# Attention and MLP mixer on one core: first loads over two queues, a later zero fill, and another step list

## The chip, the cores and the metric

The kernel runs on one core of a Trainium2 chip. The metric is device microseconds (us) of one execution; lower is better. The core has five engines that work side by side: PE (TensorE, matrix products), DVE (VectorE), ACT (ScalarE), POOL (GpSimd) and SP (SyncE, which here only issues DMAs). Each engine works off its own instructions strictly in order, and an instruction that waits holds up all that follow on its engine. Sixteen DMA engines move the data. DMAs can be issued by SP, ACT and POOL, each of which has a queue of its own.

## The reference

All inputs are bf16; S = 2048 rows, D = 512, F = 1376.

```python
xn = layernorm(x)
# A: sliding-window attention, 32 heads of 16, 8 keys at distances 0,2,..,14
q, k, v = split(xn @ wqkv)
logits[s, w] = (q[s] . k[s - 2*w]) / 4          # masked where s - 2*w < 0
s = softmax(logits) applied to v[s - 2*w], then @ wo
# B: MLP on xn
h  = gelu(layernorm(xn) @ w1)
hs = concat(h[0:128] shifted by 1 row, h[128:256] by -1, h[256:384] by 2, h[384:] by -2) @ w2
x1 = xn + hs
g  = silu(x1 + gelu(layernorm(x1) @ w3) @ w4)
out = x + s * g
```

## The kernel before

The 2048 rows are 16 tiles of 128 rows in 4 chunks of 512. A chunk's rows are dealt out so that tile i of a chunk holds every fourth row, four tiles to a chunk. Almost all of the program is a list of named steps, the string `ORDER`. Each token is a call: `v.3.3` runs `v(3, 3)`, the last number being the PSUM bank for steps that have a matrix product. Nothing reorders them: the steps are issued in the order of the list, so the list fixes the order on every engine, and the waits follow from the data, from buffers that are used again, and from the DMA completion counters, of which eight for SP and ACT are used in turn.

The steps, by engine (i is a tile, c a chunk, k a pair of tiles):

- SP, DMAs: `ldxp` loads a pair of x tiles (256 KB), `ldxc` a chunk; `ldv` and `ldw1` load one half each of v's weights and of w1 (256 KB a half), `ldqk` the q or the k half of wqkv, `ldw2`, `ldw3`, `ldw4`, `ldwo` the other weights; `xT`, `hTr`, `x1Tr`, `oTr`, `tE` are DMA transposes; `vl` loads windows of v back from DRAM; `pre` copies x to the output, `so` and `soh` store a tile or half a tile.
- DVE: `st` takes a tile's statistics (two instructions), `nm0` and `nmv` normalise; `pw` multiplies q by a shifted k; `smx`, `sms`, `smn` do the softmax; `xa` adds w2's product, `nm3` normalises for w3; `vp` multiplies v windows by the weights; `ya` adds w4's product; `sg` multiplies by the attention's output; `gb`, `fav`, `sgh`, `favh` are the last tiles' multiply and add.
- ACT: `sqw` (a first square root, which loads its table), `sq0` (square root of the variance), `ev0h` and `ev0a` (evict transposes), `ev`, `eqk`, `eh`, `eg`, `eo`, `eoT`, `ge` (evict products, some with a gelu), `si` (silu), `nm` (normalise).
- POOL: `c_zero` writes 14 rows of zeros ahead of v in DRAM by a DMA and zeroes the edges of `hT`; `c_elog`, `c_sel`, `c_ident` build constants; `rs` and `r3` are reciprocal roots for a pair; `sv` stores v by a DMA; `soa` adds a tile onto the output by a DMA.
- PE: `warmup` (products on zeros), `tr0` (transposes of the first four tiles), `v`, `w1`, `w2`, `w3`, `w4`, `wo`, `woh` (half of one), `qk`, `lg` (logits), `ws` (window sums), `oTp` (transposes).

At the start PE transposes tiles 0 and 1 (`tr0.0`, `tr0.1`), multiplies them by v's weights and by w1, then turns to tiles 2 and 3. Tiles 4 and on come transposed by DMA. At the end tiles 0 to 11 are added onto x in DRAM by `soa`, tiles 12 to 15 are finished by DVE and stored.

The list before begins so (to the first product with v's weights):

```
ldxp.s.0 c_warm c_small warmup.10.512.0 sqw c_ident kh.0 ldv.s.0 ldv.s.1 ldxp.s.1 ldw1.s.0
ldw1.s.1 c_zero st.0 ldxp.s.2 ldxp.s.3 st.1 sq0.0 ldqk.s.0 ldqk.s.1 nm0.0 sq0.1 rp.0 nm0.1
tr0.0.0 warmup.8.128.1 ev0h.0.0 ev0h.0.1 st.2 tr0.1.2 v.0.1
```

Of the kernel before, what the change touches and what calls it, by code (L numbers as in the profile page):

```python
# [18 lines left out]
tr0.0.0 warmup.8.128.1 ev0h.0.0 ev0h.0.1 st.2 tr0.1.2 v.0.1 st.3 ev0h.1.0 ev0h.1.1 sq0.2 v.1.2
ev.0 nm0.2 sq0.3 rp.1 w1.0.0 ev.1 nm0.3 rs.0 sv.0 st.5 tr0.2.1 ldxc.s.2 w1.1.2 ev0a.2 sv.1 rr.0  # L20
st.4 tr0.3.3 rs.1 v.2.1 ev0a.3 st.7 rp.2 rs.2 w1.2.4 ev.2 st.6 eh.0 v.3.3 sv.2 rp.3 rr.1 w1.3.1
nmv.4 nmv.5 ev.3 qk.0.1.5 xT.2 eh.1 sv.3 qk.0.0.3 rs.3 qk.0.3.2 eh.2 eh.3 eqk.0.1 c_elog
qk.0.4.1 qk.0.5.5 nmv.6 nmv.7 st.11 ldxc.s.3 st.10 st.8 eqk.0.3 eqk.0.5 qk.0.2.2 eqk.0.0
qk.0.6.4 eqk.0.2 st.9 eqk.0.4 qk.0.7.3 eqk.0.6 eqk.0.7 pw.0.1 rp.5 st.15 st.13 rp.4 xT.3 hTr.0
ldw2.s hTr.1 w1.4.1 v.5.4 ldwo.s.0 ev.5 w1.5.3 v.4.2 ev.4 qk.1.4.4 rs.4 sv.4 v.6.5 w1.7.2 rr.3
rr.2 eh.4 pw.0.2 kh.1 ev.6 sv.5 rs.5 nb.4 pw.0.0 st.12 eqk.1.4 eh.5 w1.6.1 qk.1.1.4 qk.1.2.3
v.7.5 hTr.2 nm.8 nm.9 w2.1.0 pw.0.3 nb.5 rp.6 eh.6 xT.4 vl.s.1.1 eh.7 st.14 rp.7 lg.0.0 rs.7
eqk.1.2 lg.0.1 ev.7 pw.0.5 w2.0.5 rs.6 eqk.1.1 nm.11 nm.10 pw.0.4 sv.7 qk.1.5.4 sv.6 xT.5
qk.1.6.3 xa.1 nb.7 qk.1.0.2 nb.6 st3s.1 eqk.1.6 hTr.3 rr.4 xa.0 ldw3.s.0 st3s.0 eqk.1.5 pw.0.6
nm.13 nm.12 nm.15 qk.1.7.0 qk.1.3.4 w2.2.5 w1.9.3 w1.8.1 eh.9 eh.8 xa.2 rr.7 hTr.4 rr.5 rq.0  # L30
w1.10.5 pw.0.7 r3.0 v.8.3 eh.10 st3s.2 nm.14 w2.3.1 nm3.0 nm3.1 eqk.1.3 w2.5.5 ev.8 qk.2.0.4
xa.3 st3s.3 eqk.1.7 eqk.1.0 xT.6 lg.0.3 rq.1 kh.2 xa.5 lg.0.2 r3.1 w2.4.2 smx.0 ldw3.s.1 sv.8
xT.7 x1Tr.0 v.10.5 qk.2.4.0 w2.6.1 eqk.2.4 nm3.3 xa.4 ex.0 w2.7.3 w1.11.2 xa.6 st3s.6 nm3.2 xa.7
qk.2.5.1 eqk.2.0 x1Tr.1 eh.11 ev.10 sv.10 rr.6 v.9.0 v.11.3 w1.13.4 eqk.2.5 ev.9 hTr.5 qk.2.7.2
w1.15.1 eqk.2.7 w1.12.0 vl.s.2.0 vl.s.0.0 ldw4.s.2 qk.2.2.2 vl.s.3.1 eh.12 pw.1.0 st3s.4 st3s.7
st3s.5 v.12.5 eqk.2.2 pw.1.3 sms.0 eh.13 v.13.0 w3.0.6.4 ev.11 hTr.6 rq.2 qk.2.1.3 pw.1.2 r3.2
sv.9 eg.0.6 eqk.2.1 ldwo.s.3 smn.0 rq.3 pw.1.1 r3.3 w3.0.1.2 qk.2.3.4 w3.0.10.3 nm3.4 eqk.2.3
tE.0 eh.15 eg.0.10 ev.13 eg.0.1 lg.1.1 lg.1.0 pw.1.7 w2.8.1 w1.14.0 w3.0.0.2 eh.14 w3.0.2.3
hTr.7 qk.2.6.0 eqk.2.6 eg.0.0 w2.10.4 nm3.6 vl.s.0.1 nm3.7 x1Tr.3 vl.s.1.0 pw.1.5 xa.8 pw.1.4
nm3.5 pw.1.6 w2.11.1 xa.10 w3.0.8.2 xa.11 qk.3.1.4 st3s.11 eg.0.8 ev.12 w2.14.1 lg.1.2 st3s.10  # L40
sv.12 lg.1.3 eqk.3.1 w2.12.4 sv.11 st3s.8 eg.0.2 smx.1 w2.9.3 ldw4.s.1 x1Tr.2 xa.9 w2.15.5 xa.14
w3.0.3.2 w3.0.9.3 xa.12 pw.2.2 qk.3.2.1 qk.3.0.4 w2.13.0 st3s.9 eqk.3.2 eqk.3.0 eg.0.3 vl.s.9.1
ldw4.s.0 rq.4 xa.15 vl.s.9.0 vl.s.3.0 ldwo.s.2 pre.s.2 qk.3.3.1 w3.0.5.2 st3s.12 qk.3.4.5 eg.0.5
pw.2.3 eqk.3.3 qk.3.5.4 st3s.14 pw.2.4 xa.13 pw.2.1 rq.5 st3s.15 v.15.1 eqk.3.5 v.14.2 ev.15
eqk.3.4 w3.1.1.0 w3.0.4.5 vp.0 st3s.13 rq.6 pw.2.0 r3.4 nm3.9 w3.0.7.1 eg.0.4 ev.14 eg.0.9
eg.0.7 ex.1 qk.3.7.4 w3.1.0.2 eg.1.0 sv.14 r3.5 nm3.10 rq.7 nm3.11 x1Tr.5 w3.1.8.1 vl.s.2.1
pre.s.1 vl.s.10.0 vl.s.10.1 w4.1.3 eqk.3.7 ldwo.s.1 kh.3 sv.15 r3.7 c_sel sms.1 w4.0.5 w4.2.4
ya.0 smn.1 r3.6 w3.1.5.5 w4.3.2 nm3.8 ya.2 ya.1 vp.1 x1Tr.4 w3.1.9.3 nm3.15 eg.1.5 ya.3 w3.1.6.4
pre.s.0 vp.3 tE.1 w3.1.7.2 eg.1.6 eg.1.1 w3.1.3.5 w3.1.4.0 eg.1.7 vp.2 lg.2.1 lg.2.0 qk.3.6.2
eg.1.8 w3.1.10.1 eqk.3.6 nm3.14 pw.2.5 pw.2.7 w3.1.2.4 eg.1.3 eg.1.10 eg.1.4 lg.2.2 pw.2.6  # L50
x1Tr.7 eg.1.2 ws.2.1 ws.1.0 ws.0.4 eg.1.9 pw.3.2 ws.3.3 eo.1 lg.2.3 eo.0 smx.2 vl.s.4.1 w4.6.0
w3.2.0.4 oTr.0 eo.2 eo.3 oTr.1 vl.s.5.1 pw.3.0 ex.2 vl.s.4.0 vl.s.6.0 vl.s.5.0 w4.5.3 vl.s.6.1
ya.6 pw.3.4 w4.7.0 w4.4.1 w3.2.3.5 sms.2 si.2 si.1 si.3 eg.2.0 eg.2.3 si.6 vl.s.7.1 vl.s.7.0
pw.3.1 pw.3.5 nm3.12 ya.4 wo.1.4 nm3.13 ya.7 w3.2.2.1 sg.1 w3.2.9.0 vp.4 ya.5 w3.2.5.4 w3.2.4.5
eg.2.9 w3.2.1.2 smn.2 x1Tr.6 w3.2.8.0 vp.5 eg.2.4 eg.2.2 eg.2.5 w3.2.10.1 w3.2.7.4 w3.2.6.5
eg.2.7 eg.2.10 eg.2.1 eg.2.8 vp.6 tE.2 vl.s.8.1 vl.s.8.0 wo.0.3 eg.2.6 wo.2.1 wo.3.0 pw.3.3 sg.2
w4.10.5 soa.2 sv.13 sg.3 vp.7 w3.3.0.0 lg.3.0 eg.3.0 lg.3.2 si.4 pw.3.6 pw.3.7 ws.4.0 ws.5.1
lg.3.1 ws.7.2 ws.6.4 eo.4 ya.10 lg.3.3 vl.s.11.1 w4.9.0 smx.3 eo.5 si.7 si.0 eo.7 si.5 eo.6
si.10 vl.s.13.1 oTr.2 vl.s.13.0 vl.s.11.0 w4.8.2 vp.9 vl.s.12.1 ex.3 oTr.3 w4.11.4 ya.8 ya.9
sms.3 ya.11 smn.3 w3.3.7.0 w3.3.5.2 w3.3.1.5 eg.3.5 vp.10 tE.3 wo.4.4 eg.3.7 eg.3.1 vl.s.14.1  # L60
vl.s.12.0 sg.0 vl.s.14.0 vp.11 w3.3.4.1 w3.3.9.2 w3.3.10.5 eg.3.10 w3.3.8.0 w3.3.3.3 w3.3.6.5
eg.3.9 eg.3.4 vp.8 w3.3.2.1 eg.3.6 eg.3.8 wo.6.2 eg.3.2 eg.3.3 wo.7.0 sg.6 vp.13 ws.10.3 ws.9.2
eo.10 ws.11.1 ws.8.5 eo.9 w4.13.3 vl.s.15.0 sg.4 vl.s.15.1 vp.12 eo.11 eo.8 wo.5.4 si.11 oTr.5
vp.14 si.9 w4.12.5 oTr.4 w4.15.1 ya.12 sg.5 si.12 si.8 sg.7 vp.15 w4.14.0 soa.1 soa.0 soa.3
soa.7 soa.5 soa.4 soa.6 ya.13 ya.15 si.13 ws.13.4 ya.14 ws.15.3 ws.12.1 ws.14.5 eo.15 wo.8.0
si.14 eo.14 wo.9.3 sg.8 eo.12 eo.13 wo.10.1 soa.8 sg.9 si.15 oTp.13.4 soa.9 sg.10 oTp.14.3
eoT.13 oTp.12.0 wo.11.5 eoT.12 oTp.15.4 eoT.14 wo.13.0 eoT.15 wo.14.3 wo.12.4 woh.15.0.1
woh.15.1.2 soa.10 sg.11 soa.11 ge.13 gb.13 ge.14 fav.13 gb.14 so.s.13 ge.12 fav.14 gb.12 so.s.14
sgh.15.0 fav.12 favh.15.0 so.a.12 sgh.15.1 soh.s.15.0 favh.15.1 soh.a.15.1
# [805 lines left out]
```

## Time and profile before

| what | value |
|---|---|
| median of 3 runs | 190.26 us (189.74 to 190.42) |
| profiled execution, its own time | 190.75 us |
| its span in the profile | 189.0 us |
| granted TensorE clock, mean | 0.996 |
| busy, share of the span | PE 97%, DVE 87%, ACT 60%, POOL 23% |
| DMA, moved | 39.25 MB, mean 208 GB/s |

How to read it: the span runs from the program's first recorded instruction to its last, and 1.75 us of the profiled execution lie around it. Times in the views count from the span's start. "[1.44 <-DMA xc<-in_A_x_dram]" behind a row says that the engine had been idle for 1.44 us before it and that the landing of x ended this idle time. A line such as L333 is a line of the kernel before. A matrix product's recorded end is modelled, so PE is best read by the starts of its rows.

### The profile page before, as it was taken

To read this page: it belongs to the slowest core of one execution; us is meant where nothing else is said; L and a number is where in the kernel's file an instruction comes from. 1 tells how busy PE (TensorE), PEld (TensorE's weight loads), DVE (VectorE), ACT (ScalarE), POOL (GpSimd) and SP (SyncE) were. 2 spreads that over 40 slices of the span, in tenths; PEclk is the share of its full clock that TensorE was granted. 3 is DMA by queue.
4 is the path that set the end of the run, shared out by engine and by line. 5 is a ranking of instruction groups with operands and counts; after the bars stand their busy time and mean duration, and the time that the engine had idled before them with its cause. 6 is when DMAs were issued, how large, how long until landed. Compare 5 with 4: busy or idle time off the path is not lost.

```text
span 189.0 us, 3685 instructions
## 1 busy us (share of the span) xinstructions
PE 182.8 (97%) x1430; PEld 87.0 (46%) x1430; DVE 165.1 (87%) x270; ACT 112.8 (60%) x189; POOL 42.7 (23%) x70
## 2 busy tenths in 40 slices
...
GB/s 164 315 352 115 199 248 141 194 238 137 233 120 286 278 64 224 222 87 190 399 162 361 274 57 134 254 401 277 189 190 95 254 335 238 210 254 106 88 106 116
DMA packets 47842, 39.25 MB, mean 208 GB/s; under 512 B 35251, under 2 KB 41889, under 8 KB 47777
## 3 DMA queue, kind: packets, MB, share of 16 engines
...
q10 hardware_dynamic: 288, 0.20, 0.3%
...
HBM read 26.41 MB, written 5.78 MB: 170 GB/s over the span
## 4 chain that ended last, share of the span: by engine, by line
PE 85%; DMA 4%; DVE 4%; issue 2%; POOL 2%; SPq 1%; ACT 1%; POOLq 0%
PE mm L668 20%; PE mm L685 18%; PE mm L443 15%; PE mm L611 8%; PE mm L496 7%; PE mm L471 6%; PE lg L543 4%; PE mm L768 4%; DMA xc<-in_A_x_dram 3%; PE mm L729 3%; POOL out_dram L835 2%; DMA out_dram<-xr 1%; DVE st L333 1%; DVE xr L775 1%; DVE xr L786 1%
## 5 line engine op out<-in xcount | busy, mean ns | idle before, releaser
L530 DVE TENSOR_TENSOR pw<-qT,kT 128x2048 bf16<-128x2048 bf16 x32 | 38.3, 1214 | 3.4 <-PE lg L543 2.4
L668 PE MATMUL mm<-x1T,w_sb 128*128 128x512 bf16 (+1 forms) x176 | 40.9, 379 | 0.0
L685 PE MATMUL mm<-w_sb,h 128*128 128x512 bf16 (+1 forms) x176 | 39.4, 379 | 0.0
L677 ACT ACTIVATE h<-mm 128x512 bf16<-128x512 f32 (+1 forms) x44 | 23.9, 602 | 23.3 <-PE mm L668 17.6
L716 DVE TENSOR_TENSOR vs<-vs,att 128x4096 bf16<-128x4096 bf16 x16 | 36.2, 2285 | 0.0
L443 PE MATMUL mm<-xnT,wqk_sb 128*128 128x512 bf16 x128 | 30.6, 379 | 0.0
L835 POOL DMA_DIRECT2D out_dram<-xr x12 | 11.0, 1117 | 74.0 <-DVE xr L775 74.0
L668 PEld LDWEIGHTS <-w_sb 128*128 128x128 bf16 (+1 forms) x176 | 17.6, 100 | 20.4
L685 PEld LDWEIGHTS <-h 128*128 128x128 bf16 (+1 forms) x176 | 16.9, 98 | 20.8 <-issue 0.4
L443 PEld LDWEIGHTS <-wqk_sb 128*128 128x128 bf16 x128 | 12.4, 98 | 15.0
L452 ACT ACTIVATE kT<-mm 128x512 bf16<-128x512 f32 x16 | 9.4, 601 | 12.1 <-PE mm L443 11.9
...
L471 PE MATMUL mm<-w2v_sb,xnT 128*128 128x512 bf16 x64 | 15.8, 379 | 0.0
L496 PE MATMUL mm<-w_sb,xnT 128*128 128x512 bf16 x64 | 15.8, 379 | 0.0
L611 PE MATMUL mm<-w2v_sb,hT 128*128 128x512 bf16 x64 | 15.7, 380 | 0.0
L768 PE MATMUL mm<-wo_sb,oT 128*128 128x512 bf16 x60 | 14.3, 379 | 0.0
L333 DVE BATCH_NORM_STATS2 st<-xc 128x6 f32<-128x512 bf16 x16 | 10.8, 676 | 3.9 <-DMA xc<-in_A_x_dram 3.9
L452 ACT ACTIVATE qT<-mm 128x512 bf16<-128x512 f32 x16 | 9.4, 605 | 7.8 <-PE mm L443 7.7
L635 POOL TENSOR_TENSOR rstd<-nmr,mhalf 128x2 f32<-128x2 f32 x8 | 9.1, 1136 | 19.8 <-DVE nmr L628 19.7
L507 ACT ACTIVATE ht<-mm,rs 128x512 bf16<-128x512 f32 x16 | 10.6, 690 | 4.4 <-PE mm L496 2.3
L696 ACT ACTIVATE xr<-xr 128x512 bf16<-128x512 bf16 x16 | 9.6, 630 | 6.0 <-DVE xr L692 6.0
L692 DVE TENSOR_TENSOR xr<-mm,xr 128x512 bf16<-128x512 f32 x16 | 10.6, 683 | 1.1 <-PE mm L685 0.9
...
## 6 DMA issues: line engine op xcount, KB each, us to landing
...
```

Source lines behind the costliest of these rows:

```text
L443: nc.tensor.matmul(pt, lhsT=wqk_sb[:, dt, nt * P : (nt + 1) * P], rhs=xnT[c][:, :, dt, :], start=(dt == 0), stop=(dt == ND - 1),)
L452: nc.scalar.activation(dst.rearrange("p (n i) -> p n i", i=TPC), mm.pop(("qk", c, nt)).rearrange("p (i n) -> p n i", i=TPC), AF.Copy,)
L471: nc.tensor.matmul(pt, lhsT=xnT[c][:, jj, dt, :], rhs=wv_sb[:, dt, :], start=(dt == 0), stop=(dt == ND - 1),)
L496: nc.tensor.matmul(pt, lhsT=xnT[c][:, jj, dt, :], rhs=w1_sb[:, dt, :], start=(dt == 0), stop=(dt == ND - 1),)
L530: nc.vector.tensor_tensor(out=pw_t[c, u], in0=q_t[c], in1=k_t[c][:, :, DIL * u : DIL * u + CH], op=ALU.mult)
L611: nc.tensor.matmul(pt, lhsT=hT[:, plane, g, p0 : p0 + P], rhs=w2_sb[:, g, :], start=(g == 0), stop=(g == ND - 1),)
L668: nc.tensor.matmul(pt[:fs, :], lhsT=w3_sb[:, dt, ft * P : ft * P + fs], rhs=x1T[c][:, :, dt, :], start=(dt == 0), stop=(dt == ND - 1),)
L677: nc.scalar.activation(h3[c, ft][:fs, :], mm.pop(("w3", c, ft))[:fs, :], AF.Gelu_apprx_tanh)
L685: nc.tensor.matmul(pt, lhsT=h3[c, ft][:fs, jj * P : (jj + 1) * P], rhs=w4_sb[:fs, ft, :], start=(ft == 0), stop=(ft == NF - 1),)
L716: nc.vector.tensor_tensor(out=vv, in0=vv, in1=att[c][:, :, H * jj : H * jj + H].unsqueeze(2).to_broadcast([P, NB * 2, DH, H]), op=ALU.mult,)
L768: nc.tensor.matmul(pt, lhsT=oT[i // 2][:, i % 2, dt, :], rhs=wo_sb[:, dt, :], start=(dt == 0), stop=(dt == ND - 1),)
L835: nc.gpsimd.dma_start(out=rows(out2, i), in_=xr[i], accum_op=ALU.add)
```

## The change

The step `ldx` is new: it loads a single x tile (128 KB). The first pair of x tiles is now loaded by `ldx.s.0` on SP and `ldx.a.1` on ACT. Of v's weights and of w1 one half each is issued by ACT (`ldv.a.1`, `ldw1.a.0`), the other by SP. `c_zero` stands behind `sv.5` now, not ahead of the first statistics. The second `warmup` has 5 products of 128 columns in place of 8. `fag` and the new `preh` are not called. The rest of the list is another order of the same steps, with other banks.

```diff
 ORDER = """
-ldxp.s.0 c_warm c_small warmup.10.512.0 sqw c_ident kh.0 ldv.s.0 ldv.s.1 ldxp.s.1 ldw1.s.0
-ldw1.s.1 c_zero st.0 ldxp.s.2 ldxp.s.3 st.1 sq0.0 ldqk.s.0 ldqk.s.1 nm0.0 sq0.1 rp.0 nm0.1
-tr0.0.0 warmup.8.128.1 ev0h.0.0 ev0h.0.1 st.2 tr0.1.2 v.0.1
+ldx.s.0 ldx.a.1 c_warm c_small ldv.s.0 ldxp.s.1 ldw1.s.1 warmup.10.512.0 ldv.a.1 c_ident
+ldw1.a.0 sqw st.0 sq0.0 st.1 nm0.0 sq0.1 nm0.1 c_elog ldxp.s.2 ldqk.s.0 ldxp.s.3 ldqk.s.1
+tr0.0.1 warmup.5.128.0 ev0h.0.0 tr0.1.2 ev0h.0.1 v.0.0
...
 """
     @step
+    def ldx(q, i):
+        if 0 not in x_c:
+            x_c[0] = rot("xc", 0, 2, [P, TPC, D])
+        qs[q].dma_start(out=xtile(i), in_=rows(x2, i))
+
+    @step
     def ldxc(q, c):
...
```

What the two lists make of each engine's order where the prediction goes into it (banks left out):

```
SP, first     before  ldxp.0 ldv.0 ldv.1 ldxp.1 ldw1.0 ldw1.1 ldxp.2 ldxp.3 ldqk.0 ldqk.1 ldxc.2 xT.2 ldxc.3 xT.3
              after   ldx.0 ldv.0 ldxp.1 ldw1.1 ldxp.2 ldqk.0 ldxp.3 ldqk.1 ldxc.2 ldw2 xT.2 xT.3 ldxc.3
ACT, first    before  sqw sq0.0
              after   ldx.1 ldv.1 ldw1.0 sqw sq0.0
PE, first     before  tr0.0 warmup tr0.1 v.0 v.1 w1.0 tr0.2 w1.1 tr0.3 v.2 w1.2 v.3 w1.3, eight qk.0
              after   tr0.0 warmup tr0.1 v.0 v.1 w1.1 tr0.2 w1.0 tr0.3 v.2 w1.2, seven qk.0, w1.3 qk.0.2 v.3
DVE, first    before  st.2 st.3 nm0.2        after  st.2 st.3 rp.0 nm0.2
POOL, first   before  c_zero rs.0 sv.0 sv.1 rs.1 rs.2 sv.2 sv.3 rs.3 c_elog
              after   c_elog kh.0 rs.0 c_sel sv.1 rs.2 sv.0 rs.1 rs.3 sv.2 rs.4 sv.3 sv.4 rs.5 sv.5 c_zero
PE, last      before  w4.13 wo.5 w4.12 w4.15 w4.14, four ws, wo.8 wo.9 wo.10 oTp.13 oTp.14 oTp.12 wo.11
                      oTp.15 wo.13 wo.14 wo.12 woh.15.0 woh.15.1
              after   w4.15 w4.14 wo.5 wo.4 w4.12 wo.10 wo.11, four ws, wo.9 wo.8 oTp.14 oTp.12 oTp.13
                      w4.13 wo.13 wo.14 oTp.15 wo.12 woh.15.0 woh.15.1
ACT, last     before  si.15 eoT.13 eoT.12 eoT.14 eoT.15 ge.13 ge.14 ge.12
              after   si.12 eoT.13 eoT.14 eoT.12 si.13 ge.13 ge.14 eoT.15 ge.12
DVE, last     before  gb.13 fav.13 gb.14 fav.14 gb.12 sgh.0 fav.12 favh.0 sgh.1 favh.1
              after   ya.13 gb.13 gb.14 fav.13 fav.14 gb.12 sgh.0 sgh.1 favh.1 fav.12 favh.0
last stores   before  soh.15.0 on SP, soh.15.1 on ACT
              after   soh.15.1 and so.12 on ACT, soh.15.0 on SP
```

More of the change, by code (lines that the diff above doesn't have):

```diff
@@ L16 @@
 ORDER = """
-ldxp.s.0 c_warm c_small warmup.10.512.0 sqw c_ident kh.0 ldv.s.0 ldv.s.1 ldxp.s.1 ldw1.s.0
-ldw1.s.1 c_zero st.0 ldxp.s.2 ldxp.s.3 st.1 sq0.0 ldqk.s.0 ldqk.s.1 nm0.0 sq0.1 rp.0 nm0.1
[L19 to L69, printed above, removed]
+ldx.s.0 ldx.a.1 c_warm c_small ldv.s.0 ldxp.s.1 ldw1.s.1 warmup.10.512.0 ldv.a.1 c_ident
@@ new lines @@
+ldw1.a.0 sqw st.0 sq0.0 st.1 nm0.0 sq0.1 nm0.1 c_elog ldxp.s.2 ldqk.s.0 ldxp.s.3 ldqk.s.1
+tr0.0.1 warmup.5.128.0 ev0h.0.0 tr0.1.2 ev0h.0.1 v.0.0 ev0h.1.0 kh.0 ev0h.1.1 v.1.1 w1.1.2 st.2
+st.3 rp.0 sq0.2 sq0.3 nm0.2 nm0.3 ev.1 rs.0 st.5 ldxc.s.2 ldw2.s tr0.2.3 w1.0.1 c_sel ev0a.2
+rp.1 st.4 tr0.3.4 v.2.3 ev0a.3 rp.2 rr.0 st.7 sv.1 rs.2 ev.0 w1.2.5 ev.2 st.6 sv.0 eh.0 rs.1
+rp.3 nmv.5 nmv.4 qk.0.0.0 qk.0.1.3 xT.2 qk.0.3.4 eh.1 rs.3 eqk.0.0 qk.0.7.1 sv.2 nmv.6 nmv.7
+qk.0.6.0 eqk.0.7 st.9 xT.3 eqk.0.1 qk.0.4.2 eqk.0.4 eqk.0.3 qk.0.5.3 rr.1 w1.3.1 ldxc.s.3 hTr.0
@@ new lines @@
+eqk.0.5 st.10 eqk.0.6 rr.2 st.8 rp.4 rs.4 qk.0.2.4 eh.2 v.3.0 eqk.0.2 v.4.5 pw.0.3 eh.3 ev.3
+v.5.1 sv.3 ev.4 st.11 rr.3 hTr.1 w1.5.0 ev.5 sv.4 nb.4 rp.5 pw.0.2 qk.1.4.5 w1.4.1 pw.0.0 pw.0.1
+nm.9 nm.8 vl.s.1.0 xT.4 qk.1.5.4 rs.5 eqk.1.5 eh.5 st.12 sv.5 c_zero qk.1.3.3 qk.1.2.2 v.6.0
+eqk.1.2 nb.5 st.13 st.14 st.15 w1.7.4 v.7.2 ev.6 eh.4 eh.7 w2.0.1 nm.11 lg.0.0 eqk.1.4 lg.0.1
+ev.7 hTr.2 vl.s.2.1 nm.10 w1.6.5 eh.6 rp.6 rs.6 xa.0 pw.0.5 pw.0.6 nb.6 w2.1.2 xa.1 rp.7 pw.0.7
+hTr.3 pw.0.4 qk.1.7.1 qk.1.6.5 nm.12 eqk.1.7 xT.5 qk.1.0.2 qk.1.1.1 sv.7 kh.1 sv.6 rs.7 lg.0.3
@@ new lines @@
+st3s.0 eqk.1.6 vl.s.3.0 ldwo.s.2 lg.0.2 rr.4 w1.9.5 nb.7 rr.6 smx.0 eqk.1.1 eqk.1.0 w1.8.2 eh.9
+w2.2.1 w2.5.5 eh.8 hTr.4 st3s.1 nm.14 nm.13 xa.5 w2.3.2 eqk.1.3 xa.2 rq.0 xT.6 v.9.4 rr.5 pw.1.1
+w1.10.5 w1.11.1 v.8.3 ldw3.s.1 w2.4.0 eh.10 ev.9 nm.15 xT.7 ev.8 r3.0 sv.8 st3s.5 st3s.2 eh.11
+v.10.4 xa.4 xa.3 hTr.5 sv.9 ev.10 qk.2.4.1 eqk.2.4 ex.0 w2.6.2 w2.7.4 nm3.1 vl.s.2.0 pw.1.3
+st3s.3 v.12.1 ldw3.s.0 qk.2.2.0 xa.6 rq.1 w1.13.2 st3s.4 nm3.0 x1Tr.0 r3.1 xa.7 eh.13 nm3.2
+pw.1.0 nm3.3 eqk.2.2 rr.7 ev.12 qk.2.0.3 w1.12.4 rq.2 sms.0 r3.2 qk.2.3.5 qk.2.7.2 eh.12 sv.12
@@ new lines @@
+kh.2 w1.14.1 eh.14 eqk.2.0 w2.9.4 hTr.6 eqk.2.3 qk.2.6.0 x1Tr.1 w1.15.3 pw.1.4 st3s.6 eh.15
+pw.1.2 eqk.2.6 qk.2.1.5 st3s.7 qk.2.5.1 hTr.7 smn.0 w2.8.0 eqk.2.5 pre.s.1 lg.1.0 lg.1.1 pw.1.5
+vl.s.0.1 tE.0 ldw4.s.1 ldwo.s.3 v.11.1 vl.s.1.1 xa.8 xa.9 w2.11.3 vl.s.3.1 st3s.8 w3.0.10.0
+st3s.9 rq.4 eqk.2.1 eqk.2.7 ev.11 w3.0.2.4 xa.11 st3s.11 pw.1.6 w2.10.1 w3.0.6.2 ldw4.s.2
+ldw4.s.0 w2.15.3 xa.15 xa.10 nm3.4 rq.3 st3s.10 ldwo.s.0 w2.12.5 eg.0.6 eg.0.2 w3.0.8.4 w3.0.4.3
+w2.13.1 eg.0.4 w3.0.0.2 eg.0.0 eg.0.8 w3.0.5.3 sv.10 r3.3 eg.0.10 nm3.5 rq.5 r3.5 xa.13 x1Tr.2
@@ new lines @@
+w3.0.7.1 pw.2.0 w2.14.4 eg.0.7 eg.0.5 sv.11 w3.0.3.0 v.14.3 xa.14 r3.4 w3.0.9.4 w3.0.1.1 eg.0.1
+xa.12 nm3.6 nm3.7 pw.1.7 v.15.5 vp.1 qk.3.6.2 vl.s.0.0 ev.15 v.13.1 vl.s.10.1 x1Tr.3 vl.s.9.0
+st3s.12 st3s.14 pre.s.0 qk.3.7.5 eg.0.9 vp.2 ev.13 lg.1.3 sv.15 sv.13 lg.1.2 eg.0.3 qk.3.5.0
+qk.3.2.1 eqk.3.5 eqk.3.6 ev.14 sv.14 eqk.3.7 pw.2.3 w4.1.4 smx.1 nm3.9 pw.2.1 st3s.13 w4.3.5
+w4.2.3 vp.0 ex.1 qk.3.4.2 st3s.15 w4.0.0 ya.2 nm3.8 rq.7 nm3.10 ya.1 w3.1.4.3 nm3.11 ya.3 x1Tr.5
+pre.s.2 w3.1.9.4 rq.6 eg.1.4 ya.0 r3.6 kh.3 r3.7 pw.2.2 sms.1 x1Tr.4 vl.s.10.0 eg.1.9 w3.1.8.5
```

29 lines of the change are left out of this document (26 added, 3 removed).

## The prediction

> **What bounds the kernel now.** I read the page first, its busy shares and its slices, then the busy time by stretch, then the chain of waits, and last the timeline at both ends.
>
> ```profile
> PE 182.8 (97%) x1430; PEld 87.0 (46%) x1430; DVE 165.1 (87%) x270; ACT 112.8 (60%) x189; POOL 42.7 (23%) x70
> ```
>
> ```profile
> 0.00:10.11 10.11, 8.43 (x38) 3.61 (x39) 5.08 (x18) 4.70 (x12) 3.10 (x14) 1.00 0.74 249
> 10.11:60.00 49.89, 49.87 (x354) 23.47 (x355) 42.90 (x114) 36.26 (x60) 18.07 (x30) 1.00 0.86 199
> 60.00:120.00 60.00, 60.00 (x538) 29.07 (x537) 56.81 (x78) 30.18 (x53) 10.37 (x14) 1.00 0.88 210
> 120.00:170.00 50.00, 50.00 (x399) 23.77 (x397) 48.07 (x43) 32.81 (x51) 4.19 (x5) 1.00 0.94 245
> 170.00:189.00 19.00, 14.55 (x107) 7.07 (x104) 12.23 (x21) 8.85 (x16) 6.99 (x8) 0.96 0.67 104
> ```
>
> The columns are the stretch, its length, and the busy time of PE, PEld, DVE, ACT and POOL, then the granted clock and the DMA's share and rate. From 10.11 to 170 us PE has no idle time to speak of (159.87 of 159.89 us). DVE is close behind it: 147.78 us. So the span is three things: when PE's unbroken run begins, whether it stays unbroken, and what follows its end. The chain shows what sets the beginning:
>
> ```profile
> 2.15 5.68 DMA xc<-in_A_x_dram
> 7.83 0.02 issue
> 7.85 0.71 DVE st L333
> ...
> 10.11 0.40 PE mm L356 x4
> ```
>
> The second pair of x tiles, issued at 2.15, lands at 7.83; 2.28 us later, after two tiles' statistics and one tile's normalising, PE transposes tile 2. From there the chain is PE almost to the end.
>
> **The front.** SP's rows give the issues and the view of each tile's transfers the times to landing: x pair 0 at 0.73, 2.9 us; v's halves at 1.18 and 1.64, 3.1 and 5.5 us; x pair 1 at 2.15, 5.68 us; w1's halves at 2.66 and 3.14, 5.8 and 6.0 us. So they land at 3.6, 4.3, 7.15, 7.83, 8.5 and 9.15: a step of 256 KB costs 0.67 us, but v's second half took 2.87 us after the first, 2.2 us lost, and pair 1 stands behind it on the same queue.
>
> In the new list pair 1 is third on SP, behind 128 KB of x and half of v. ACT's queue holds the other x tile, v's second half and half of w1. If the two queues share the DMA engines evenly, 1.15 to 1.28 MB have moved when pair 1 is in, where it was 1.02: 4.5 to 5 steps of 256 KB. Without lost time that is 3.6 + 3.5 x 0.67 = 5.9 us to 3.6 + 4 x 0.67 = 6.3 us; with the 2.2 us lost as before, 8.5 us. No row of before shows two such queues filled at once. I take 7.4, midway: the half of v that lost the time no longer stands ahead of pair 1, but shares the engines with it.
>
> `tr0.2` follows 2.28 us behind the landing, and 0.1 more, since `rp.0` (0.16 us, partly overlapped) is now ahead of `nm0.2`. That gives 7.4 + 2.38 = 9.8, against 10.11: **-0.3 us**. There is a floor: before, `w1.0` started at 8.83 and its four products need 0.22 us each, so PE was through with all it had at 9.70; three fillers less (8 took from 6.27 to 6.78, so 0.06 each) make this 9.5. A landing ahead of 7.1 therefore brings no more than -0.6; a landing at 8.5 costs +0.8.
>
> ACT now issues three DMAs ahead of its table load. At SP's 0.4 to 0.5 us each the load (1.28 us) and the first root (0.20) end at 3.6 instead of 2.2; the root for tile 0 starts at 4.56, so it is hidden. If ACT and SP had to take turns at issuing, they would end at 4.9 and `tr0.0` would be 0.35 us late, still ahead of the gate at tile 2: nothing in either case. `w1.1`, now the first product with w1, needs both halves of w1, 1.54 MB in both lists, so by about 9.15; its second pair of products would start at about 8.9, 0.25 us too early, which the wait for tile 2 covers.
>
> The single zero DMA and the two memsets (0.73, 0.35 and 0.35 us on POOL) leave a place where POOL idled for 3.16 us afterwards. Behind `sv.5` (about 26 us) they end near 28; the first reader, `w2.0`, has 28.8 us of PE work ahead of it and starts at about 31: nothing.
>
> **The middle.** Here I counted the busy time ahead of each step on its own engine, in the old list and in the new one, with the profile's durations (four products of 512 columns 0.86 us, a `w4` 2.38, a `pw` 1.14, a `vp` 2.2), and kept the idle time that the engine had gathered by then. The transposed inputs stay 6 us and more ahead of their readers in both lists. What is tight is DVE ahead of PE:
>
> - `xa.9` frees the bank of `w3.0.2`: 57.4 us of DVE work and 11.1 us of idle time make 68.5; PE, with 64.5 us of work and 3.3 us of idle time, wants it at 67.8. Short by 0.7 us.
> - `pw.3.7` ahead of `lg.3.3`: 128.7 + 13.2 = 141.9 against 137.8 + 3.8 = 141.6. Short by 0.3.
> - `vp.15` ahead of `ws.15`: 159.8 + 14.3 against 169.9 + 4.2. Level.
>
> These are not added up: a stall at the first gives time to the next. Against them stands that DVE idles less early on:
>
> ```profile
> 17.59 0.87 DVE L410 TENSOR_SCALAR xr<-xc,mv,rs 128x512 bf16<-128x512 bf16 x2 [2.45 <-POOL rs L386]
> ...
> 22.70 1.23 DVE L530 TENSOR_TENSOR pw<-qT,kT 128x2048 bf16<-128x2048 bf16 x1 [1.04 <-ACT kT L452]
> ```
>
> The 2.45 us are `rs.3`, which stood on POOL behind two `sv` that waited for ACT; it now stands ahead of them. Most of this goes into a longer wait at `pw.0.3`, which needs all eight `qk.0`. But the eighth now stands ahead of `v.3`, so that 18.4 instead of 19.5 us of PE work precede it: `pw` starts 0.9 us earlier with 0.5 us less DVE work done, a gain of 0.4, and at `xa.0`, behind `w2.0`, it is 8.9 instead of 9.5 us of idle time. These 0.6 us cover all but **+0.1 us** of the 0.7. If DVE gathers its old idle time after all, it is +0.7; below zero it can't go, since PE has no idle time here to win.
>
> **The end.**
>
> ```profile
> 181.98 0.60 ACT L782 ACTIVATE vt<-mm 128x512 bf16<-128x512 f32 x1
> ...
> 182.61 0.42 DVE L786 TENSOR_TENSOR xr<-vt,xr 128x512 bf16<-128x512 bf16 x1 [1.02 <-ACT vt L782]
> ...
> 186.00 0.29 DVE L807 TENSOR_TENSOR xr<-xc,xr 128x256 bf16<-128x256 bf16 x1
> ```
>
> Before, `ge.13` was evicted at 181.98, and from 182.61 to 186.29 DVE worked without a break; `soh.15.1` was issued at 186.37 and landed 1.6 us later. In the new list `w4.13` comes after the last window sums. With PE as dense as before, its last product is issued by 184.4 (`woh` starts at 183.51, plus 0.86). Behind `w4.13` stand three `wo`, an `oTp` and two halves: 3 x 0.86 + 0.23 + 0.86 = 3.7, so `w4.13` is through at 180.7. Then `ya.13` starts 0.28 us later (`sg.8` did so behind `wo.8`) and takes 0.69, `si.13` starts at 181.7, and `ge.13`, next on ACT (start to start 0.5), at 182.2. `ge.14`, `eoT.15` and `ge.12` follow at 182.7, 183.2 and 183.7; each stands behind `si.13`, and `woh.15.0` waits about 0.35 us for `eoT.15`. DVE: `gb.13` at 182.83, `gb.14` at 183.33 behind `ge.14`, then the other eight by the spacing of before (whole tiles 0.40 to 0.46, halves 0.20 to 0.42), to 186.56: 0.27 later. The last store is SP's half tile, issued at 186.65; halves landed 1.6 us (ACT) and 1.9 us (SP) after issue, so 188.2 to 188.5 against 187.94: +0.3 to +0.6, **+0.4 us** taken.
>
> **The sum.** -0.3 + 0.1 + 0.4 = +0.2 us. On the profiled execution, 190.75 (189.0 of span and 1.75 around it), that is 190.95; the median of the runs is 0.49 lower, so 190.26 + 0.2 = **190.5 us**. What a measurement here can tell from no change is about 0.5%, 0.95 us: no change is 189.3 to 191.2.
>
> **Rivals.** *A, slower: the second pair of x comes late.* Place: the wait of `st.2`. Every us of landing past 7.7 comes out at the end, since PE has nothing else to do. With the 2.2 us lost again and both queues sharing, 8.5 us: +0.8 + 0.1 + 0.4 = +1.3, 191.6. It decides from a landing at about 8.2. For it: the rows show the lost time; against it: one slow transfer on one queue need not hold up the other. The Trainium skill speaks for it: DMA: Bandwidth & Descriptors, section Issuing engines are not separate DMA queues, says that DMAs of all issuing engines run on the same 16 DMA engines and interleave, and that several issuers save only the time of issuing. By that rule alone the sum is this rival's; no run shown here has both queues filled. Chance 0.2.
>
> *B, slower: DVE does not keep its lead.* Place: `w3.0.2`, `w3.0.4` and `lg.3.3`. With all old idle time and 0.6 us more from steps in an unlucky order, PE stalls 1.3 us: -0.3 + 1.3 + 0.4 = +1.4, 191.7. Against it: the counts above. Chance 0.12.
>
> *C, faster: loads without lost time, and the end not longer.* Pair 1 by 6.8, and tile 0, a transfer of 128 KB and no longer 256, half a step (0.3 us) earlier, so that the floor falls from 9.5 to 9.2: -0.9, or 189.3 to 189.4, at the edge of what can be told. For it: the zero DMA on POOL, issued at 1.50 and landed at 5.50, lies exactly over the slow stretch, and is gone from it. The Trainium skill, same page, section Latency and other measured facts, says that two of the 16 DMA engines are usually slower and guesses at POOL's descriptor rings as the reason; by that the loss would go with the zero DMA. Chance 0.16, 0.1 of it beyond the edge.
>
> *D, the split does nothing:* the halves land when they did, pair 1 at 7.8. Then +0.1 + 0.1 + 0.4 = +0.6, 190.9: inside the forecast.
>
> **Numbers.** Forecast, with D in it, 0.5; A 0.2, B 0.12, C 0.16; 0.02 for what I don't see, put with faster. Faster by over 0.5%: 0.1 of C and this, 0.12; slower: A and B, 0.32; within 0.5%: the forecast and the rest of C, 0.56. The forecast's own range is 189.8 to 191.0. For 8 in 10 it reaches down to C's 189.3 and up past A and B, to 192.2, where both would meet (+0.8 + 0.7 + 0.4 = 1.9).
>
> **What would show it.** Right: `st.2` waits less than 1.44 us and `tr0.2` starts near 9.8; PE without idle time from there to `lg.3.3`; `rs.3` no longer DVE's longest wait; `gb.13` near 182.5, DVE through 0.3 later in relation to PE's last product. Wrong: a landing of pair 1 past 8.2 or ahead of 6.5; PE waits on `xa` or `pw` of more than 0.5 us in sum; a last store that follows PE's end no later than before.

## The result, and the profile after

The changed kernel takes 190.56 us (median of 22 runs, 190.11 to 191.39), the kernel before 189.88 us (median of 22 runs beside them, 189.74 to 190.50): ratio 1.0032, 95% interval 1.0022 to 1.0042. It is slower by 0.68 us, or 0.4%. That is less than the bound of 0.5% of the forecast, but with 1 outside the interval it is a difference.

The profiled execution of after took 190.29 us, its span 188.5 us. That is 0.5 us *less* than the profiled execution of before, and the reason is the latter: its 190.75 us are above all 22 timed runs of the same kernel. So the two profiles may not be subtracted as they stand. First the page's busy line and the busy time by stretch of after, the stretches cut at the start of tile 2's transposes as in the prediction (length, PE, PEld, DVE, ACT, POOL, granted clock, DMA share and rate):

```profile
PE 181.0 (96%) x1412; PEld 86.2 (46%) x1427; DVE 164.1 (87%) x270; ACT 110.6 (59%) x187; POOL 43.0 (23%) x70
```

```profile
0.00:9.33 9.33, 7.32 (x36) 3.06 (x36) 5.08 (x17) 4.17 (x11) 3.32 (x19) 1.00 0.81 270
9.33:60.00 50.67, 50.41 (x353) 23.91 (x359) 44.89 (x115) 37.85 (x62) 20.57 (x30) 1.00 0.93 221
60.00:120.00 60.00, 59.74 (x533) 29.05 (x537) 55.51 (x79) 31.50 (x54) 8.47 (x10) 1.00 0.73 190
120.00:170.00 50.00, 49.79 (x395) 23.62 (x397) 48.20 (x45) 28.88 (x48) 2.71 (x4) 1.00 0.89 244
170.00:188.50 18.50, 13.78 (x101) 6.61 (x100) 10.39 (x19) 8.16 (x16) 7.94 (x9) 0.99 0.69 107
```

The first stretch is 0.78 us shorter than in the profile of before. In the three middle ones PE is busy for all but 0.73 us, and that is not idle time: 1412 of 1430 products are on record, and where one is missing the trace shows a space of two products (0.43 us) and no wait. The view of waits names none for PE after tile 0's transposes. The front, in the chain of waits:

```profile
1.66 5.32 DMA xc<-in_A_x_dram
6.98 0.02 issue
7.00 0.70 DVE st L339
...
9.33 0.40 PE mm L362 x4
```

The second pair of x (pair 1) was issued at 1.66 and landed at 6.98; tile 2's transposes start 2.35 us later. SP and ACT did not take turns. Both issue their first three DMAs in the same half microseconds, as the timelines of ACT and of SP have it:

```profile
0.74 0.41 ACTq L212 DMA_DIRECT2D xc<-in_A_x_dram  x1
1.17 0.47 ACTq L240 DMA_DIRECT2D w2v_sb<-in_A_wqkv_dram  x1
1.67 0.52 ACTq L247 DMA_DIRECT2D w_sb<-in_B_w_dram  x1
```

```profile
0.74 0.39 SPq L212 DMA_DIRECT2D xc<-in_A_x_dram  x1
1.19 0.42 SPq L240 DMA_DIRECT2D w2v_sb<-in_A_wqkv_dram  x1
1.66 0.47 SPq L227 DMA_DIRECT2D xc<-in_A_x_dram  x1
```

DVE's two long waits of the prediction did what it said: the one on POOL's root shrank from 2.45 to 0.90 us, the one ahead of `pw.0.3` grew from 1.04 to 1.98.

```profile
15.25 0.74 DVE L416 TENSOR_SCALAR xr<-xc,mv,rs 128x512 bf16<-128x512 bf16 x2 [0.90 <-POOL rs L392]
...
20.98 1.23 DVE L536 TENSOR_TENSOR pw<-qT,kT 128x2048 bf16<-128x2048 bf16 x1 [1.98 <-ACT qT L458]
```

The end: DVE's timeline of after, then the last stores of after in ACT's and SP's timelines, then those of before:

```profile
181.88 0.91 DVE L792 TENSOR_TENSOR xr<-vt,xr 128x512 bf16<-128x512 bf16 x2 [1.18 <-ACT vt L788]
...
185.12 0.28 DVE L813 TENSOR_TENSOR xr<-xc,xr 128x256 bf16<-128x256 bf16 x1
```

```profile
185.35 0.44 ACTq L849 DMA_DIRECT2D out_dram<-xr  x1
...
185.46 0.33 SPq L819 DMA_DIRECT2D out_dram<-xr  x1
```

```profile
185.70 0.33 SPq L813 DMA_DIRECT2D out_dram<-xr  x1
...
186.37 0.34 ACTq L813 DMA_DIRECT2D out_dram<-xr  x1
```

DVE ends at 185.40, 176.07 us after the start of tile 2; before it was 176.19 (186.29 - 10.11). So DVE is through 0.1 us *earlier* in relation to tile 2. But from DVE's end to the end of the span it is now 3.11 us and was 2.67. Two stores are issued last, a whole tile on ACT (landed 2.0 us after issue) and half a tile on SP (2.07); before, the last one was half a tile on ACT, landed 1.56 us after issue. This holds beyond these two profiles: in all eight below that end with half a tile on ACT the span ends 2.63 to 2.67 us behind DVE, in the six with the new last stores 3.11 to 3.20.

### The profile page after: what moved, and what is told of

Its sections match the earlier page's. It is cut to its first block, busy times and chain, and to the rows that moved or that the text cites. A ratio compares the mean times of both kernels' runs of the same rounds, so it can differ in the third digit from the quotient of the medians.

```text
span 188.5 us, 3657 instructions
## 1 busy us (share of the span) xinstructions
PE 181.0 (96%) x1412; PEld 86.2 (46%) x1427; DVE 164.1 (87%) x270; ACT 110.6 (59%) x187; POOL 43.0 (23%) x70
## 4 chain that ended last, share of the span: by engine, by line
PE 90%; DVE 3%; DMA 3%; issue 1%; ACT 1%; SPq 0%; DVEq 0%; ACTq 0%
PE mm L674 20%; PE mm L691 20%; PE mm L449 15%; PE mm L617 7%; PE mm L502 7%; PE mm L477 6%; PE mm L774 5%; PE lg L549 4%; PE mm L735 4%; DMA xc<-in_A_x_dram 3%; DVE st L339 1%; ACT vt L788 1%; DVE xr L792 0%; DVE xr L698 0%; DVE xr L808 0%
## 5 line engine op out<-in xcount | busy, mean ns | idle before, releaser
L641 POOL TENSOR_TENSOR rstd<-nmr,mhalf 128x2 f32<-128x2 f32 x8 | 7.2, 897 | 37.2 <-DVE nmr L634 30.0
L624 DVE TENSOR_TENSOR xr<-mm,xr 128x512 bf16<-128x512 f32 x16 | 10.5, 683 | 3.5 <-PE mm L617 3.5
L698 DVE TENSOR_TENSOR xr<-mm,xr 128x512 bf16<-128x512 f32 x16 | 10.7, 681 | 3.2 <-PE mm L691 3.2
L749 ACT ACTIVATE o<-mm 128x512 bf16<-128x512 f32 x16 | 8.9, 595 | 7.3 <-issue 4.9
L392 POOL TENSOR_TENSOR rs<-ve,mhalf 128x4 f32<-128x4 f32 (+1 forms) x8 | 9.4, 1207 | 13.9 <-DVE ve L384 8.0
```

## A sum that holds for every profile

Between the start of tile 2's transposes and the end PE has no idle time that varies, so an execution's time is that start plus a part that only the list sets. This table is read from the profiles ("rest" is time minus start); its right half is all timed runs of the kernel (6 to 22) against the kernel before on the same chip, whose medians there are 189.88 to 190.01 us. The ratio is an estimate of its own over these runs and not the quotient of the two medians; for e7 that quotient would be 1.0073.

| kernel | pair 1 landed | tile 2 starts | time | rest | median, all runs | ratio, 95% interval |
|---|---|---|---|---|---|---|
| before (first profile) | 7.83 | 10.11 | 190.75 | 180.64 | 189.88 | |
| b0_again: before | 7.18 | 9.48 | 190.09 | 180.61 | 189.92 | 0.9998 (0.9990 to 1.0007) |
| e3: before, late zero | 6.74 | 9.39 | 189.94 | 180.55 | 190.03 | 1.0005 (0.9993 to 1.0017) |
| e1: before, split loads | 6.79 | 9.23 | 189.74 | 180.51 | 190.68 | 1.0039 (1.0028 to 1.0051) |
| e1b: e1 again | 6.95 | 9.23 | 189.82 | 180.59 | 190.41 | 1.0019 (1.0004 to 1.0035) |
| e5: e1, late zero | 6.77 | 9.82 | 190.32 | 180.50 | 190.21 | 1.0014 (0.9999 to 1.0029) |
| after | 6.98 | 9.33 | 190.29 | 180.96 | 190.56 | 1.0032 (1.0022 to 1.0042) |
| a0_again: after | 7.42 | 9.78 | 190.76 | 180.98 | 190.95 | 1.0055 (1.0036 to 1.0074) |
| a1_again: after | 7.48 | 9.83 | 190.81 | 180.98 | 190.80 | 1.0037 (1.0023 to 1.0050) |
| e2: after, loads on SP | 7.03 | 9.69 | 190.71 | 181.02 | 190.73 | 1.0038 (1.0023 to 1.0053) |
| e6: e2, early zero | 6.45 | 9.35 | 190.40 | 181.05 | 190.48 | 1.0023 (1.0011 to 1.0034) |
| e7: after, pair 1 first | 5.12 | 9.64 | 190.58 | 180.94 | 191.30 | 1.0053 (1.0035 to 1.0071) |
| e4: after, old end, first try | 6.93 | 9.37 | 191.42 | 182.05 | 191.46 | 1.0095 (1.0065 to 1.0124) |
| e4b: after, old end | 8.11 | 10.46 | 190.90 | 180.44 | 190.38 | 1.0016 (1.0004 to 1.0029) |

The rest is 180.50 to 180.64 in the six profiles with the old list and 180.94 to 181.05 in the six with the new list and its end: 0.4 us, with no overlap. The start of tile 2 scatters from one execution to the next by more than that. Taking the rest off the medians gives the usual start: 9.3 for the kernel before, 9.6 to 10.0 for the changed one.

## The experiments

**b0_again and a0_again: both kernels once more, unchanged.**

> The kernel before, unchanged, for a second profile. Three theories on why the span of the changed kernel is 0.5 us shorter in its profile (188.5 against 189.0) and its median 0.7 us longer (190.56 against 189.88). Chance: the first profile of before caught an execution with a late second x pair (landing at 7.83); most executions have it near 7.0, so the span here is 188.0 to 188.3, tile 2 is transposed at 9.2 to 9.5. Split costs: the same for this kernel, landing near 6.7 to 7.0. Split gains: the landing is at 7.6 to 8.0 again and the span near 189.0.

> The changed kernel, unchanged, for a second profile. Chance: landing of the second x pair between 6.8 and 7.6, span 188.3 to 189.3, no stall of PE between tile 2 and the end. Split costs: landing typically later than in the kernel before, 7.2 to 7.6, span near 188.8. Split gains: landing 7.0 again, span 188.5.

Measured: 189.92 and 190.95 us. The second profile of before shows its usual front. DVE's and PE's timelines:

```profile
7.20 0.69 DVE L333 BATCH_NORM_STATS2 st<-xc 128x6 f32<-128x512 bf16 x1 [0.81 <-DMA xc<-in_A_x_dram]
```

```profile
6.84 1.93 PE L471 MATMUL mm<-w2v_sb,xnT 128*128 128x512 bf16 x8
8.62 1.03 PE L496 MATMUL mm<-w_sb,xnT 128*128 128x512 bf16 x4
9.48 0.39 PE L356 MATMUL mm<-ident,xr 128*128 128x128 bf16 x4
```

Pair 1 lands at 7.18, DVE waits 0.81 us for it and not 1.44, and PE goes from v and w1 to tile 2 without a space: 12 products at 0.22 us behind the first product with v's weights, 6.84 + 2.64 = 9.48. So tile 2 starts at the later of two times: pair 1's landing + 2.3 us, and the first product with v's weights + 2.6 us. In every profile of the table this rule gives the start to 0.06 us. In the first profile of before it was the landing; in this one the two are level. The 7.83 of the first profile was an outlier, an execution in which one of the 16 reports of v's second half came 1.1 us after the others. (The trace holds 16 reports of completion for each transfer; the last of them is the landing.)

**e1_split_in_before: the old list, only the first loads split.**

```diff
-ldxp.s.0 c_warm c_small warmup.10.512.0 sqw c_ident kh.0 ldv.s.0 ldv.s.1 ldxp.s.1 ldw1.s.0
-ldw1.s.1 c_zero st.0 ...
+ldx.s.0 ldx.a.1 c_warm c_small ldv.s.0 ldxp.s.1 ldw1.s.1 warmup.10.512.0 ldv.a.1 c_ident
+ldw1.a.0 sqw kh.0 c_zero st.0 ...
```

> The list of before with the first loads alone changed: x tile 0, half of v, x pair 1, half of w1 on SP; x tile 1, half of v, half of w1 on ACT; the zero DMA and all else as before. Chance (the loads make no difference, the new end of the list costs 0.3 to 0.6 us): time as before, within 0.2 us, 189.9. Split costs: 0.3 to 0.5 us above before. Split gains: 0.8 us below before.

Measured: 190.68 us, ratio 1.0039, with a spread of 189.74 to 191.35, where before has 189.7 to 190.4. The split alone costs time.

**e2_sp_in_after: the new list, the first loads back on SP.**

```diff
-ldx.s.0 ldx.a.1 c_warm c_small ldv.s.0 ldxp.s.1 ldw1.s.1 warmup.10.512.0 ldv.a.1 c_ident
-ldw1.a.0 sqw st.0 ...
+ldxp.s.0 c_warm c_small ldv.s.0 ldv.s.1 ldxp.s.1 ldw1.s.0 ldw1.s.1 warmup.10.512.0 c_ident
+sqw st.0 ...
```

> The changed kernel with the first loads back on SP alone, in the order of before (pair 0, v, v, pair 1, w1, w1); the zero DMA stays late, the list stays new. Chance: as the changed kernel, 190.5 within 0.2 us. Split costs: 0.3 to 0.5 us faster than the changed kernel, 190.1. Split gains: 0.8 us slower than it, 191.3.

Measured: 190.73 us, 0.2 us under the changed kernel beside it (190.95), but 0.81 above before. The rest, 181.02, is 0.45 of that. The front of its profile shows a second source of scatter, in PE's timeline, first of e2 and then of a0:

```profile
6.17 0.74 PE L327 MATMUL mm<-warm 128*128 128x128 bf16 x5
6.70 0.56 PE L362 MATMUL mm<-ident,xr 128*128 128x128 bf16 x4
7.10 1.89 PE L477 MATMUL mm<-w2v_sb,xnT 128*128 128x512 bf16 x8
8.83 1.03 PE L502 MATMUL mm<-w_sb,xnT 128*128 128x512 bf16 x4
9.69 0.39 PE L362 MATMUL mm<-ident,xr 128*128 128x128 bf16 x4
```

```profile
5.80 0.44 PE L327 MATMUL mm<-warm 128*128 128x128 bf16 x5
6.09 0.40 PE L362 MATMUL mm<-ident,xr 128*128 128x128 bf16 x4
```

The same five fillers start 0.11 us apart in e2 and 0.06 in a0: PE still runs at half its rate there. In e2 it comes to full rate at 7.05 us, and so v's first product is at 7.10 and tile 2 at 9.69, though pair 1 (7.03) would have allowed 9.38.

**e3_late_zero: the old list, only `c_zero` moved.**

```diff
-ldw1.s.1 c_zero st.0 ...
+ldw1.s.1 st.0 ...
...
-... ev.6 sv.5 rs.5 ...
+... ev.6 sv.5 c_zero rs.5 ...
```

> The list of before with one edit: c_zero (the zero DMA and two memsets on POOL) stands behind sv.5 instead of ahead of the first statistics. Loads stay on SP. Profiles so far say: execution time = start of tile 2's transposes + 180.6 us in the old list, + 181.0 us in the new one. Theory Zero helps (POOL's small DMA disturbs the first loads, so without it they land sooner): below 189.8 us, and a narrower spread. Theory Zero hides (its absence early is what made the new front slow and scattered, since the new list with SP loads had 190.17 to 191.68): 190.3 to 190.5. Theory Zero is nothing: 189.9, ratio 1.000 within 0.001, spread of 0.7 us as before.

Measured: 190.03 us, ratio 1.0005 with 1 inside the interval. POOL's early zero DMA costs the start nothing, and moving it brings nothing.

**e5_split_late_zero: e1 with e3's edit.**

> The list of before with the first loads split over SP and ACT (as in e1) and c_zero behind sv.5. With e1 (split, zero early: 190.68), the kernel before (SP, zero early: 189.92) and e3 (SP, zero late) it fills a table of two by two. Theory Split alone costs (two queues filled at once make the second pair of x land later and more scattered, whatever POOL does): 190.6 to 190.8, spread over 1.2 us. Theory Three queues (the cost of e1 comes from POOL's zero DMA meeting two filled queues; without it the changed kernel's front holds, 9.6 us for tile 2): 9.6 - 0.05 + 180.6 = 190.1 to 190.2.

Measured: 190.21 us, ratio 1.0014, 0.18 us above e3 beside it. So the split costs less here than in e1, and the two theories are not told apart, since e1 and e5 ran on two chips; e1b, below, is for that.

**e6_sp_early_zero_in_after: e2 with `c_zero` back ahead of `st.0`.**

> The changed kernel with the first loads back on SP in the old order (as in e2) and c_zero back ahead of the first statistics; the rest is the new list. Theory Front undone (both undone, the loads are as before and only the end's 0.35 us are left): 189.9 + 0.35 = 190.2 to 190.35, spread 0.7 us. Theory New list (something else in the new list's first steps scatters the start: the order of q's and k's weights and the x pairs, five filler products instead of eight, w1.1 first): as e2, 190.7, spread 1.5 us.

Measured: 190.48 us (190.15 to 190.90), 0.47 above before. Minus its rest, 181.05, tile 2 usually starts at 9.4: the front of before within 0.1 us, and what is left is the new list's rest. The spread is halved against e2. Whether that is the zero DMA or the chip stays open; in the old list (e3) the zero DMA did nothing.

**e4_old_end_in_after: the changed kernel, its end in the old manner, first try.**

```diff
 w4.12.2
...
-... wo.10.3 wo.11.4 ...
+... w4.13.3 ...
...
 ws.15.1
+ya.12
...
+ya.13
...
-... oTp.13.1 w4.13.3 eoT.13 ...
+... oTp.13.5 wo.10.1 eoT.13 ...
...
+... wo.11.2 ... eoT.12 si.12 si.13 eoT.15 ...
...
-sgh.15.0 sgh.15.1 favh.15.1 fav.12 soh.a.15.1 favh.15.0 so.a.12 soh.s.15.0
+sgh.15.0 fav.12 favh.15.0 so.a.12 sgh.15.1 soh.s.15.0 favh.15.1 soh.a.15.1
```

> The changed kernel with the front and middle as they are and only the steps after ya.15 put as in the old list: w4.13 ahead of the last window sums, ya.13 and si.13 long before the end, wo.10 and wo.11 behind the window sums in its place, eoT.15 ahead of ge.13, the two half tiles stored last in the old order. Theory End (0.35 us of the difference are the chain from w4.13 to the last store): 0.3 to 0.4 us under the changed kernel, so 190.2 to 190.6, ratio 1.0015 to 1.0035; in the profile the span is the start of tile 2's transposes plus 178.8 to 178.9 us, where the changed kernel has 179.2. Theory Front only (the end is covered by something else): as the changed kernel, 190.6 to 190.95, and 179.2 us.

Measured: 191.46 us. The edit brought a wait of its own. ACT's and PE's timelines:

```profile
180.35 1.08 ACT L768 ACTIVATE oT<-mm 128x512 bf16<-128x512 bf16 x2 [1.35 <-PE mm L774]
```

```profile
181.48 2.75 PE L774 MATMUL mm<-wo_sb,oT 128*128 128x512 bf16 x12 [1.17 <-ACT oT L768]
```

`eoT.14` writes into a buffer that `wo.11` still reads, `wo.11` had been put late, and PE stood 1.17 us for `eoT.14`. It says nothing of the theory.

**e4b_old_end: the old end without that wait.** `w4.13` ahead of the window sums as in e4; behind them, in the old order, `wo.8 wo.9 wo.10`, three transposes, `wo.11`, `oTp.15 wo.13 wo.14 wo.12` and the halves; the old order of the last steps.

> The changed kernel with the old end again, mended: e4 had put wo.10 and wo.11 behind the transposes, so that eoT.14 had to wait for wo.11 to free its buffer, and PE stood for 1.2 us ahead of wo.14. Now w4.13 is ahead of the window sums, and behind them the old order stands (wo.8, wo.9, wo.10, three transposes, wo.11, oTp.15, wo.13, wo.14, wo.12, the halves). Theory End: PE without a wait from tile 2 to the halves, last store 0.3 to 0.35 us earlier in relation to tile 2: span = start of tile 2's transposes + 178.8 to 178.9 us (changed kernel 179.2), median 0.3 to 0.4 under the changed kernel beside it. Theory Front only: 179.2 and the changed kernel's median.

**a1_again: the changed kernel beside it.**

> The changed kernel once more, unchanged, beside e7, e4b and e1b on the same chip. Profiles so far: time = start of tile 2's transposes + 181.0 us (180.6 in the old list); that start is 9.1 us at the earliest. Theory Late pair (the slow executions are those in which the second pair of x lands past 7 us): where the profiled execution is above 190.6, its pair 1 lands past 7.2 us and DVE's wait for it is over 1.1 us. Theory Clock (the slow ones are those in which TensorE comes to full speed late, seen in the spacing of the filler products, 0.11 instead of 0.06 us): pair 1 lands by 7.1 and the first product with v's weights starts past 7.0 us.

Measured: e4b 190.38, a1 190.80 us; ratios 1.0016 and 1.0037. The end is worth 0.4 us. In the profiles the rest falls from 180.98 to 180.44, and the span minus tile 2's start from 179.17 to 178.64. DVE's last row of e4b and its last store on ACT's queue:

```profile
186.19 0.29 DVE L813 TENSOR_TENSOR xr<-xc,xr 128x256 bf16<-128x256 bf16 x1
```

```profile
186.55 0.36 ACTq L819 DMA_DIRECT2D out_dram<-xr  x1
```

From tile 2 to DVE's end it is 176.02 us in e4b (186.48 - 10.46) and 176.08 in a1: level. The 0.5 us lie behind DVE's end: 2.63 us to the end of the span against 3.13. Even e4, where DVE ends 1.6 us later behind its own wait, has 2.64 us, and its last stores are the old ones. So it is the last stores that cost time and not the chain from `w4.13`. A run with the stores alone undone was not made, but the profiles leave the chain 0.06 us.

For the front, a1 is the profile that was wanted, an execution like the median. DVE's timeline of a1 and PE's:

```profile
7.51 0.69 DVE L339 BATCH_NORM_STATS2 st<-xc 128x6 f32<-128x512 bf16 x1 [1.35 <-DMA xc<-in_A_x_dram]
```

```profile
9.83 0.40 PE L362 MATMUL mm<-ident,xr 128*128 128x128 bf16 x4 [0.42 <-DVE xr L351]
```

Pair 1 landed at 7.48, PE had been at full rate since 4.9 us at the latest and stood for tile 2: here it was the late pair. So it was in a0 (7.42, 190.76 us) and, most of all, in the profile of e4b, where the landing at 8.11 made 190.90 us of a kernel whose median is 190.38.

**e1b_split_again: e1 on another chip.**

> e1 once more (the old list with only the first loads split), for a second profile and on another chip, since e1 and e5 were measured on two. Theory Split alone costs: ratio 1.003 to 1.004 again, 190.5 to 190.8. Theory Chips (the cost was that chip's): nearer to e5, 190.1 to 190.3, ratio 1.001.

Measured: 190.41 us, ratio 1.0019, spread 189.72 to 191.07. Between the two theories' figures: the split alone costs 0.14 to 0.39% in three comparisons (e1, e1b, e5), with the interval of one reaching 1.

**e7_pair1_first: the changed kernel, pair 1 ahead of v's half on SP.**

```diff
-... c_small ldv.s.0 ldxp.s.1 ldw1.s.1 ...
+... c_small ldxp.s.1 ldv.s.0 ldw1.s.1 ...
```

> The changed kernel with one edit: SP issues the second pair of x ahead of its half of v's weights. The pair should land 0.7 to 1.3 us earlier, near 6 us, v's half on SP later, near 6.0 to 6.3 us. Theory Late pair: tile 2 no longer waits for its loads, so the start of tile 2's transposes goes to PE's own floor of 9.1 to 9.5 in nearly all executions: median 190.2 to 190.4, highest under 190.9. Theory Clock or other loads: the scatter stays, median within 0.1 of the changed kernel's beside it, highest above 191. If v's half now comes too late, the first product with v's weights starts past 6.8 us and everything is later by that.

Measured: 191.30 us, slower than the changed kernel beside it by 0.5 us in the medians and 0.3 in the ratios. In the profile (190.58 us) pair 1 landed at 5.12, but v's half on SP only at 6.92. PE's timeline:

```profile
7.05 1.89 PE L477 MATMUL mm<-w2v_sb,xnT 128*128 128x512 bf16 x8 [0.17 <-ACT xnT L370]
8.78 1.03 PE L502 MATMUL mm<-w_sb,xnT 128*128 128x512 bf16 x4
9.64 0.39 PE L362 MATMUL mm<-ident,xr 128*128 128x128 bf16 x4
```

ACT's evictions of the transposes began at 6.40; in a1 they began at 6.12 and the first product followed 0.44 us later, so here it could have been at 6.84. It started at 7.05, 0.13 us behind the landing of v's half, though the row names ACT. So the gate has moved from pair 1 to v. Theory Late pair, as it was put, is wrong: an earlier pair does not bring the start to its floor, because v must be in by then as well. The median lies 0.7 us above this profile, and which load is late in those executions was not seen.

## Why the prediction was right, and where only by luck

**The median** came out at 190.56 where 190.5 was forecast, but that closeness is luck. The sum said +0.2 us; against the kernel before as measured beside it, it was +0.68 (+1.03 and +0.88 in a0 and a1). The +0.2 was put on a median of three runs, 190.26, which was 0.38 above the 189.88 of 22: one error made up for the other. What held is the middle; the size of the end held too, but through other terms than those of the sum, so in part by luck.

**The front: -0.3 forecast, about +0.3 measured** (0.26 from the result's medians less the rests, 0.6 and 0.5 in the same way from a0 and a1). The landing came out as taken, though 7.4 was the middle between two bounds and not derived: 6.98, 7.42, 7.48, 6.93 and 8.11 in the five profiles with this front (after, a0, a1, e4, e4b), median 7.42. The way from landing to tile 2 was right too (2.38 taken, 2.35 measured). What failed is the other side of the subtraction, "against 10.11". The first profile's start was an outlier; the usual one of before is 9.3 (189.9 - 180.6). The prediction gave the sign of it away when it noted that the profile was 0.49 above the median: against 22 runs it is 0.87, and nearly all of that was this start. The 2.2 us lost by v's second half belong to the same execution: in the other four profiles with SP alone the same loss is 0.05 to 1.6 us.

That the split alone costs time is shown in the old list by e1 and e1b; in the new list e6 undoes the front's loss, but e2, also with SP alone, does not. What it does to the loads is in the 16 reports of pair 1's landing. The eighth of them came at 5.53 to 5.84 us in the five profiles with SP alone, and at 5.93 to 6.32 in the eight with two queues and pair 1 behind v's half: 0.4 us later on the mean (6.09 against 5.69), although pair 1 was issued 0.5 us earlier. In the same time two queues move more (1062 to 1194 KB from 3.5 to 7.0 us; 835 to 1053 with one, POOL's zeros left out), but what they move ahead of pair 1 is partly w1, which stood behind it on the one queue. That is the sharing that the prediction counted as 1.15 to 1.28 MB for 1.02. But the eighth report is not the landing: the last came at 6.45 to 7.83 in the five and at 6.77 to 8.11 in the eight, and these overlap. The Trainium skill's rule that issuing engines are not separate DMA queues (DMA: Bandwidth & Descriptors) fits these landings as far as the transfers interleave; that two queues moved more bytes here goes beyond it. It was put with rival A, whose 8.5 us did not come; in its smaller form, 0.4 us in the eighth report, it is the likeliest source of the front's 0.3; with the scatter of the last reports this is argued and not shown.

**The middle: +0.1 forecast, 0 measured** up to the last products; rival B, a DVE that loses its lead, is refuted by every profile of the new list, none of which has a wait of PE from tile 3 to `wo.12`, but for e4 with its own edit.

**The end: +0.4 forecast, 0.4 measured** (0.42 between the means of the rest, and 0.42 between the medians of a1 and e4b), but made up otherwise. `woh.15.0` starts 173.54 us after tile 2, where it was 173.40: the forecast wait, net 0.14 and not 0.35 us. `gb.13`, `ge.14` and the others do stand behind `si.13`, yet DVE's end moved 0.1 us ahead and not 0.27 back. The loss came from the step that the prediction priced lowest, the last stores: 0.44 us more from DVE's end to the span's. The prediction followed the half tile on SP alone; in e2 and e6 it is the whole tile on ACT that lands last, 2.15 us after issue. Which of size, queue and closeness in time makes these stores slower was not tested.

**c_zero and ACT's issues: nothing forecast, nothing measured.** e3 has 1.0005; ACT's table load starts at 2.22 and its first root ends at 3.71, ahead of its first use. With e3, rival C's idea that the zero DMA makes the slow transfer falls: the late reports are there without any DMA of POOL in flight, as in after and a1. So the guess at POOL's descriptor rings, which the Trainium skill makes for two slower engines in Latency and other measured facts on the same page, does not explain the late reports of this kernel; whether they are those two engines' the trace does not tell. C's other half came true and paid nothing: tile 0 landed 0.2 us sooner (3.35 in after, 3.57 in b0) and v's first product started at 6.50 instead of 6.84, but pair 1 held tile 2 back.

**Still open.** Both profiles of e1 caught executions near its fastest (189.74 and 189.82), so that what makes its median 0.5 to 0.8 us slower is argued from the landings and not seen. Nor is it settled why e2, with SP's loads, scattered as widely as the split kernels on its chip. A kernel with e6's front and e4b's end was not run; by the table it would take 9.4 + 180.44 = 189.84 us, an estimate, not to be told from before.
